# Windowed attention and a Strassen-type maxout layer on one core: the order of the attention groups on TensorE, a pinned instruction order, and later subtractions

## The chip, the core and the metric

One NeuronCore of a Trainium2 chip runs the whole program. The metric is the device time of one execution in microseconds (us), the median of several runs; for the kernel before it is 850.38 us (three runs, 847.42 to 852.41).

The engines are named as in the profile: PE is TensorE (matmuls and transposes), PEld its weight loads, DVE is VectorE, ACT is ScalarE, POOL is GpSimd, SP issues DMAs. PSUM is the memory into which PE writes and from which DVE and ACT read; POOL works on SBUF alone.

## The reference

Batch 8, 8 heads, 576 positions, head size 64; then 4608 tokens, model width 512, hidden width 768.

```python
def _attn_ref(q, k, v):
    scores = scale * np.matmul(q, k.transpose(0, 1, 3, 2))
    bias = slopes[:, None, None] * (-np.abs(rel).astype(np.float32))[None, :, :]
    mask = (rel >= 0) & (rel < window)          # window = 128
    scores = np.where(mask, scores + bias[None], -1000000000.0)
    attn = np.exp(scores - np.max(scores, axis=-1, keepdims=True))
    attn = attn / (np.sum(attn, axis=-1, keepdims=True) + 1e-09)
    return np.matmul(attn, v)

def _moe_ref(x, w1, w2, w3, w_out):             # x: heads side by side, (B*S, 512)
    h = np.maximum(np.maximum(x @ w1, x @ w2), x @ w3)
    return h @ w_out
```

## The kernel before, in words

**Attention.** A task is one batch and one pair of heads, and has five blocks of queries, four of 128 rows and one of 64. Two consecutive blocks form a group. For a group PE does three kinds of work. `products` (L248 to L264) writes the scores into the PSUM tile `ps_s`, in matmuls of 64 rows by 64 columns of the array, four side by side. `turn` (L314 to L342) transposes the normalised probabilities `p` into the PSUM tile `pt`, in the full 128x128 array (64x128 for the block of 64 rows). `mix` (L344 to L370) multiplies with v into `ps_x`, in 128x64 pieces side by side (64x64 for the block of 64 rows); blocks 0 and 1 make one run of `mix`, blocks 2, 3 and 4 the other. Between them DVE merges the two halves of the window and adds the bias (L277, L289), ACT takes the exponential and normalises (L293, L312), ACT copies `pt` out of PSUM (L325, L331, L334), and POOL cuts the copy into the two triangles (L335, L339). So PE gets ten groups in a batch.

**The maxout layer.** Each of the 11 products of a batch (9 for the three weight matrices, 2 for the output) is done by a scheme with 7 multiplications of blocks instead of 8, in two-part (high and low) arithmetic. One such multiplication is a unit (`unit`, L482 to L522), 77 in a batch: 6 matmuls of 128x128 by 288 columns for the first 63, 9 for the 14 of the output. They are all issued at L510. Units write to three PSUM buffers `ps_m` in turn, which DVE (L468, L473, L476) and ACT (L519) empty.

When the three matrices of a third `p` of the hidden layer are done, `factors_h` (L420 to L450) forms the differences of its blocks for the output product: a subtraction on DVE (`sub`, L391) and a `cut` into high and low part, a cast on ACT (L387) and a subtraction on POOL (L388). For the third part DVE does the first two. The last subtraction, `sub(b10, b10, t)` at L449, overwrites b10, and so waits until POOL has finished the cut of b10 that L448 asked for.

**Order.** The code makes a list of events, each with a time in steps of attention (L525 to L578), and issues them sorted by time. A `mix` stands at .01 of its step, a `turn` at .02, a `products` at .03. `later` (L379) puts the steps of `factors_h` on a list by unit number, and `unit` issues those that are due. Behind that stands a scheduler: it takes the issued instructions and sets a fixed order for each engine by its own estimate of when operands are ready, so an instruction may come to stand earlier or later than it was issued.

**Weights.** They are prepared during batch 0, kept in DRAM and streamed from there in later batches (`stream`, L216), through a ring of two buffers for each half, by DMAs that POOL issues (L221).

Of the kernel before, what the change touches and what calls it, by code (L numbers as in the profile page):

```python
# [18 lines left out]
LAG_T, LAG_X = 4, 6  # L19
# [10 lines left out]
def attention_maxout_kernel(  # L30
# [11 lines left out]
    nc = tc.nc  # L42
# [7 lines left out]
    NB = (S + P - 1) // P  # L50
# [165 lines left out]
    def stream():  # L216
        nonlocal streamed
        n, a = divmod(streamed, 2)
        if n < 9 * B and prepared == 120 and ahead(n, a):
            place(n, a)  # L220
            nc.gpsimd.dma_start(wts[n, a], keep[n % 9][a])  # L221
            streamed += 1


    tasks = [(b, hp) for b in range(B) for hp in range(NP)]
    qkt, vt = {}, {}
# [21 lines left out]
    def products(s):  # L248
        whole = s < NP * NB and s % 4 == 2
        ps = [ps_m.tile([P, 512], F32, name=f"ps_m{j}") for j in range(2)] if whole else [scores[:, j] for j in range(2)]  # L250
        for a, (t, i) in enumerate(steps[s:s + 2]):
            n = rows[i]
            banks[t, i] = [x[:, a * 2 * P:(a + 1) * 2 * P] for x in ps], None if whole else a
            for j in range(2):
                for d in range(0, n, D):
                    q0 = i * P + d
                    k0, k1 = (0, P) if i == 0 else ((i - 1) * P, i * P + n) if whole else (q0 - P, q0 + D)
                    o = a * 2 * P + k0 - (i - 1) * P
                    nc.tensor.matmul(  # L259
                        ps[j][d:d + D, o:o + k1 - k0],  # L260
                        lhsT=qkt[t][j * D:(j + 1) * D, 0, q0:q0 + D],
                        rhs=qkt[t][j * D:(j + 1) * D, 1, k0:k1],
                        start=True, stop=True, skip_group_check=True,
                    )  # L264

    def score(t, i):
        b, hp = tasks[t]
# [46 lines left out]
    def turn(s):  # L314
        pt = ps_t.tile([P, 2, 2, P], F32, name="pt")
        two = steps[s:s + 2]
        for a, (t, i) in enumerate(two):
            n = rows[i]
            p = pn.pop((t, i))
            for j in range(2):  # L320
                nc.tensor.transpose(out=pt[:, a, j, :n], in_=p[:n, j], identity=ident[:n, :n])  # L321
        r = s_p.tile([P, 2, 2, P], F32, name="pr", bufs=2)
        whole = all(i and rows[i] == P for _, i in two)
        if whole:
            nc.scalar.copy(out=r, in_=pt)  # L325
        for a, (t, i) in enumerate(two):
            n = rows[i]
            w = pp_p.tile([P, 2, 2, P], F32, name="pp")
            pp[t, i] = w
            if i == 0:  # L330
                nc.scalar.copy(out=w[:, :, 0, :n], in_=pt[:, a, :, :n])  # L331
                continue
            if not whole:
                nc.scalar.copy(out=r[:, a, :, :n], in_=pt[:, a, :, :n])  # L334
            nc.gpsimd.affine_select(  # L335
                out=pp[t, i - 1][:, :, 1, :n], in_=r[:, a, :, :n], pattern=[[0, 2], [-1, n]],
                compare_op=ALU.is_gt, fill=0.0, base=0, channel_multiplier=1,
            )
            nc.gpsimd.affine_select(  # L339
                out=w[:n, :, 0, :n], in_=r[:n, a, :, :n], pattern=[[0, 2], [1, n]],  # L340
                compare_op=ALU.is_ge, fill=0.0, base=0, channel_multiplier=-1,
            )  # L342

    def mix(t, i):  # L344
        b, hp = tasks[t]
        if i == 0:
            xp[t] = ps_x.tile([P, 1024], F32, name="ps_x")
        x, vv, w = xp[t], vt[t], pp[t, i]
        n = rows[i]
        m = rows[i + 1] if i + 1 < NB else 0  # L350
        parts = []
        c0 = i * P
        if m == 0 or (c0 // 512 != (c0 + P) // 512):
            parts.append((0, n, c0))
            if m:
                parts.append((P, P + m, c0 + P))
        else:
            parts.append((0, P + m, c0))
        for a, e, c in parts:
            for j in range(2):  # L360
                nc.tensor.matmul(  # L361
                    x[j * D:(j + 1) * D, c:c + e - a],
                    lhsT=vv[:n, i, j * D:(j + 1) * D],
                    rhs=w[:n, j].rearrange("p a b -> p (a b)")[:, a:e],
                    start=i == 0 or (c % 512 == 0 and a == P), stop=True, skip_group_check=True,
                )
        if i == NB - 1:
            if hp % 2 == 0:
                xk[b, hp // 2] = xk_p.tile([P, 2, S], F32, name=f"xk{hp // 2}")
            nc.scalar.copy(out=xk[b, hp // 2][:, hp % 2], in_=x[:, :S])  # L370
# [8 lines left out]
    def later(when, what, *args):  # L379
        todo.append((when, what, args))  # L380
        todo.sort(key=lambda x: x[0])
# [38 lines left out]
    def factors_h(b, p, ij, when):  # L420
        b00, b01, b10, b11 = [hq.get((p, x)) for x in ((0, 0), (0, 1), (1, 0), (1, 1))]

        def cut(k, src):
            if p < 2:
                if p == 0:
                    hs[b, k] = hs_p.tile([P, 2, 2, C], F32R, name="hs")
                t = hs[b, k][:, p]
            else:
                if k in (0, 2, 4, 5):
                    hs[b, "at"] = hs_p.tile([P, 2, 2, C], F32R, name="hs2", bufs=4)  # L430
                t = hs[b, k, 2] = hs[b, "at"][:, k in (1, 3, 6)]
            split((t[:, 0], t[:, 1]), src, nc.vector if p == 2 and k < 2 else nc.gpsimd)

        if ij == (0, 0):
            t = hq["t", p] = t_p.tile([P, C], F32, name="t")
            sub(t, b01, b00)
            later(when, cut, 0, b00)
            later(when, cut, 1, t)
        elif ij == (1, 1):
            t = hq["t", p]  # L440
            later(when, sub, t, b11, t)
            later(when, sub, b01, b11, b01)
            later(when, cut, 2, t)
            later(when, cut, 3, b11)
        elif ij == (1, 0):
            t = hq["t", p]
            later(when, cut, 5, b01)
            later(when, cut, 4, b10)  # L448
            later(when, sub, b10, b10, t)  # L449
            later(when, cut, 6, b10)  # L450

# [30 lines left out]
    def unit(u):  # L482
# [24 lines left out]
            part_of[n, k] = ps_m.tile([P, 512], F32, name=f"ps_m{u % 3}")[:, :C]  # L507
        ps = part_of[n, {2: 0, 5: 0, 6: 0, 3: 1}.get(k, k)]
        for i, (lt, rt) in enumerate(pairs):
            nc.tensor.matmul(  # L510
                ps, lhsT=lt, rhs=rt, start=i == 0 and k in (0, 1, 4), stop=i == len(pairs) - 1,
                skip_group_check=True,
            )
        if g < 9:
            used.add((at, k))
        stream()
# [11 lines left out]
    def at(when, what, *args):  # L528
        events.append((when, len(events), what, args))
# [3 lines left out]
    for t, (b, hp) in enumerate(tasks):  # L533
        for i in range(NB):
# [7 lines left out]
            c = s - (t * NB + i) % 2  # L542

            if s == c:
                at(c + LAG_T + 0.02, turn, t * NB + i)
                at(c + 0.03, products, t * NB + i)
            at(s + 0.04, score, t, i)
            if i % 2 or i + 1 == NB:
                at(s + 0.9, sums_of, t, i)
                at(s + 1.3, normalise, t, i)  # L550
            e = t * NB + next(min(e + 1, NB - 1) for e in GROUPS if e >= i)
            at(e - e % 2 + shift[b] + LAG_X + 0.01, mix, t, i)

    ready = [n_steps * (b + 1) - 2 + LAG_X + 0.05 + shift[b] for b in range(B)]
    when = ready[0]
# [13 lines left out]
    for s in range(1, n_steps + LAG_X):  # L569
        at(s + 0.2, weights, 2)  # L570

    load(0)
    nc.sync.dma_start(ident, c_ident)
    slopes(0)
# [42 lines left out]
```

## Time and profile before

| what | value |
|---|---|
| median of the runs | 850.38 us |
| the profiled execution | 846.03 us, of which the span of the program's instructions is 844.3 us |
| busy share of the span | PE 92%, PEld 80%, DVE 68%, ACT 64%, POOL 37% |
| mean granted clock of TensorE | 0.961 |
| instructions | 17942, of them 6272 matmuls |
| moved by DMA | 184.78 MB, 219 GB/s |

The span falls into three parts: to about 195 us attention of batch 0, preparation of the weights and the first units; then six batches of about 94.4 us, in which a batch's units run beside the next batch's attention; and from about 766 us the last batch's units alone.

In the timeline a row merges instructions of one line that follow each other: start, time from the first start to the last end, engine, line, operation, tiles, the form of the first of them, and their number. Matmuls overlap in their ends, so the time of a section is read as the difference of two rows' starts. The scores are multiplied in two passes, so that 8 instructions of the order are 16 in the trace; the same holds for `mix`. A bracket at the end of a row is the idle time before it, with what ended it.

### The profile page before, as it was taken

To read this page: it belongs to the slowest core of one execution; us is meant where nothing else is said; L and a number is where in the kernel's file an instruction comes from. 1 tells how busy PE (TensorE), PEld (TensorE's weight loads), DVE (VectorE), ACT (ScalarE), POOL (GpSimd) and SP (SyncE) were. 2 spreads that over 40 slices of the span, in tenths; PEclk is the share of its full clock that TensorE was granted. 3 is DMA by queue.
4 is the path that set the end of the run, shared out by engine and by line. 5 is a ranking of instruction groups with operands and counts; after the bars stand their busy time and mean duration, and the time that the engine had idled before them with its cause. 6 is when DMAs were issued, how large, how long until landed. Compare 5 with 4: busy or idle time off the path is not lost.

```text
span 844.3 us, 17942 instructions
## 1 busy us (share of the span) xinstructions
PE 780.3 (92%) x6272; PEld 674.3 (80%) x6272; DVE 570.0 (68%) x1830; ACT 544.5 (64%) x1790; POOL 310.3 (37%) x544
## 2 busy tenths in 40 slices
PE   4767778799999999999999999999999999999997
PEld 2335666589888988888888988889888988889897
DVE  5788989996666845775557845775657846583552
ACT  6898888876666856676556756675657756642332
POOL 1212141442354415452345415451345415440431
PEclk9865989799999999999999999999999999999999
DMA  6742568673887558873787558873787557764851
GB/s 230 278 168 70 220 230 305 210 257 125 262 277 249 195 171 261 277 253 118 239 273 252 196 175 267 275 255 110 245 281 240 194 187 244 230 223 153 296 205 56
DMA packets 43401, 184.78 MB, mean 219 GB/s; under 512 B 4784, under 2 KB 13744, under 8 KB 34096
## 3 DMA queue, kind: packets, MB, share of 16 engines
q0 software_dynamic: 18144, 115.61, 41.7%
q1 hardware_dynamic: 25024, 67.97, 22.8%
q8 instruction: 49, 0.80, 0.4%
q14 instruction: 40, 0.33, 0.1%
q10 hardware_dynamic: 144, 0.07, 0.0%
HBM read 157.68 MB, written 25.95 MB: 217 GB/s over the span
## 4 chain that ended last, share of the span: by engine, by line
PE 68%; DVE 8%; issue 8%; POOL 6%; ACT 6%; DMA 3%; SPq 0%; POOLq 0%; ACTq 0%; DVEq 0%
PE ps_m L510 53%; PE ps_x L361 6%; PE ps_s L259 5%; PE pt L321 4%; POOL hs L388 3%; DMA wt<-keep 2%; POOL pp L339 1%; POOL pp L335 1%; ACT p L293 1%; ACT hs L387 1%; DVE hs L158 1%; DVE t L473 1%; DMA hs<-in_w_all 1%; DVE hs L144 1%; DVE xs L388 1%
## 5 line engine op out<-in xcount | busy, mean ns | idle before, releaser
L510 PE MATMUL ps_m<-xs,wt 128*128 128x288 f32 x3024 | 440.8, 302 | 19.9 <-DVE hq L476 7.6
L510 PEld LDWEIGHTS ps_m<-xs,wt 128*128 128x128 f32 x3024 | 414.6, 191 | 46.6 <-issue 12.2
L519 ACT COPY t<-ps_m 128x288 f32<-128x288 f32 x264 | 101.2, 392 | 92.3 <-PE ps_m L510 91.9
L335 POOL TENSOR_SCALAR_AFFINE_SELECT pp<-pr 128x256 f32<-128x256 f32 (+1 forms) x128 | 53.9, 421 | 263.0 <-ACT pr L334 175.9
L510 PE MATMUL ps_m<-hs,ow 128*128 128x288 f32 x1008 | 144.5, 299 | 3.2 <-POOL hs L388 2.4
L293 ACT ACTIVATE p<-s,st 128x128 f32<-128x128 f32 (+1 forms) x320 | 126.7, 399 | 27.9 <-DVE st L289 27.2
L510 PEld LDWEIGHTS ps_m<-hs,ow 128*128 128x128 f32 x1008 | 136.0, 188 | 9.6 <-POOL hs L388 5.9
L388 POOL TENSOR_TENSOR hs<-hq,hs 128x288 fp32r<-128x288 f32 x112 | 101.3, 914 | 88.3 <-ACT hs L387 88.1
L221 POOL DMA_DIRECT2D wt<-keep x126 | 69.8, 554 | 150.3 <-PE ps_m L510 148.8
L312 ACT ACTIVATE p<-p,st 128x128 f32<-128x128 f32 (+1 forms) x320 | 108.6, 399 | 20.6 <-DVE st L305 20.0
L289 DVE CUSTOM_DVE_ANT_0 s<-ps_s,bias 128x128 f32<-128x128 f32 (+1 forms) x300 | 77.5, 283 | 25.9 <-PE ps_s L259 19.0
L473 DVE TENSOR_TENSOR t<-ps_m,t 128x288 f32<-128x288 f32 x144 | 65.1, 453 | 43.5 <-PE ps_m L510 27.3
L361 PE MATMUL ps_x<-pp,v 128*64 128x256 f32 (+3 forms) x768 | 85.6, 338 | 7.3 <-POOL pp L335 6.6
L277 DVE COPY_PREDICATED ps_s<-prev,ps_s 128x256 f32<-128x256 uint8 x120 | 50.6, 421 | 56.9 <-PE ps_s L259 55.7
L259 PE MATMUL ps_s<-qk 64*64 64x192 f32 (+1 forms) x1080 | 71.3, 346 | 11.5 <-DVE st L289 7.4
L321 PE MATMUL pt<-ident,p 128*128 128x128 f32 (+1 forms) x320 | 62.0, 295 | 17.3 <-ACT p L312 15.2
L387 ACT CAST hs<-hq 128x288 fp32r<-128x288 f32 x120 | 50.3, 433 | 39.0 <-DVE hq L474 26.0
L361 PEld LDWEIGHTS ps_x<-pp,v 128*64 128x64 f32 (+1 forms) x768 | 46.7, 140 | 35.1 <-POOL pp L335 11.8
L321 PEld LDWEIGHTS pt<-ident,p 128*128 128x128 f32 (+1 forms) x320 | 37.2, 145 | 42.7 <-ACT p L312 20.9
L474 DVE TENSOR_TENSOR hq<-t,hq 128x288 f32<-128x288 f32 x144 | 67.4, 475 | 2.7
L259 PEld LDWEIGHTS ps_s<-qk 64*64 64x64 f32 x1080 | 40.1, 141 | 26.9 <-issue 13.2
L293 ACT ACTIVATION_READ_ACCUMULATOR p<-s,st 128x1 f32 (+1 forms) x320 | 61.5, 192 | 0.0
(56 smaller groups left out, 719.2 us busy)
## 6 DMA issues: line engine op xcount, KB each, us to landing
wt<-keep POOLq DMA_DIRECT2D x63, 1024.0 KB, 7.2
wt<-keep POOLq DMA_DIRECT2D x63, 768.0 KB, 4.6
qk<-in_qk SPq DMA_DIRECT2D x31, 576.0 KB, 5.8
hs<-in_w_all SPq DMA_DIRECT2D x24, 512.0 KB, 6.6
v<-in_v SPq DMA_DIRECT2D x32, 320.0 KB, 4.8
keep<-wt SPq DMA_DIRECT2D x9, 1024.0 KB, 4.7
outT<-t SPq DMA_DIRECT2D x64, 144.0 KB, 1.8
keep<-wt SPq DMA_DIRECT2D x9, 768.0 KB, 5.2
```

The source lines that it names most:

```text
L221: nc.gpsimd.dma_start(wts[n, a], keep[n % 9][a])
L259: nc.tensor.matmul(ps[j][d:d + D, o:o + k1 - k0], lhsT=qkt[t][j * D:(j + 1) * D, 0, q0:q0 + D], rhs=qkt[t][j * D:(j + 1) * D, 1, k0:k1], s ...
L289: nc.vector.tensor_tensor_reduce(out=s[:n], in0=ps[j][:n, P:2 * P], in1=(bias if i else bias0)[:n, 2 * hp + j, :], scale=-0.125, scalar=3. ...
L293: nc.scalar.activation(p[:n, j], s[:n], AF.Exp, bias=st[:n, 0, a, j:j + 1], scale=-1.0, accum_out=st[:n, 1, a, j:j + 1])
L312: nc.scalar.activation(p[:n, j], p[:n, j], AF.Copy, scale=st[:n, 2, a, j:j + 1])
L321: nc.tensor.transpose(out=pt[:, a, j, :n], in_=p[:n, j], identity=ident[:n, :n])
L361: nc.tensor.matmul(x[j * D:(j + 1) * D, c:c + e - a], lhsT=vv[:n, i, j * D:(j + 1) * D], rhs=w[:n, j].rearrange("p a b -> p (a b)")[:, a:e ...
L388: e.tensor_tensor(out=lo, in0=src, in1=hi.bitcast(F32), op=ALU.subtract)
L473: nc.vector.tensor_tensor(out=s, in0=ps, in1=e, op=ALU.add)
L474: nc.vector.tensor_tensor(out=h, in0=s, in1=h, op=ALU.max)
L510: nc.tensor.matmul(ps, lhsT=lt, rhs=rt, start=i == 0 and k in (0, 1, 4), stop=i == len(pairs) - 1, skip_group_check=True,)
L519: nc.scalar.copy(out=e, in_=ps)
```

## The change

It has three parts. First, from the step in which batch 2's products with v begin, every PE instruction is tied to the one issued before it (`tc.keep_in_program_order`), so the scheduler can't move it. Second, the times of the attention events are changed: within a step, `mix` comes at .001, `products` at .002, `turn` at .003, so that the transposes follow the scores. Third, in `factors_h` the differences and cuts of block (1,1) are issued 2 units later for the first two thirds, and the last subtraction and its cut 5 units later (2 for the last third). The matmuls themselves, their number and their shapes don't change.

```diff
+    fixed = False
+
+    def pe(ins):
+        if fixed:
+            tc.keep_in_program_order(ins)
...
         elif ij == (1, 1):
             t = hq["t", p]
+            when += 2 * (p < 2)
             later(when, sub, t, b11, t)
...
             later(when, cut, 5, b01)
             later(when, cut, 4, b10)
+            when += 5 if p < 2 else 2
             later(when, sub, b10, b10, t)
             later(when, cut, 6, b10)
...
             if s == c:
-                at(c + LAG_T + 0.02, turn, t * NB + i)
-                at(c + 0.03, products, t * NB + i)
+                at(c + 0.002, products, t * NB + i)
+                at(c + LAG_T + 0.003, turn, t * NB + i)
...
-            at(e - e % 2 + shift[b] + LAG_X + 0.01, mix, t, i)
+            at(e - e % 2 + shift[b] + LAG_X + 0.001, mix, t, i)
...
+    def fix():
+        nonlocal fixed
+        fixed = True
+
+    at(2 * n_steps + LAG_X + shift[2], fix)
```

All `nc.tensor` calls of `products`, `turn`, `mix` and `unit` are wrapped in `pe(...)`. The lines of the changed kernel are numbered 6 to 13 higher: scores L265, transposes L327, products with v L367, units L518, subtraction L397.

What it moves, engine by engine, is seen in two places of batch 4. The first is PE around the sixth run of `mix` in that batch, before:

```order
L510 MATMUL ps_m_7363<-xs,wt_7203 128x288 x6
L361 MATMUL ps_x<-pp,v 64x256
L510 MATMUL ps_m_7229<-xs,wt_7156 128x288 x6
L510 MATMUL ps_m_7352<-xs,wt_7203 128x288 x6
L510 MATMUL ps_m_7363<-xs,wt_7203 128x288 x6
L510 MATMUL ps_m_7421<-xs,wt_7266 128x288 x6
L361 MATMUL ps_x<-pp,v 64x256
L361 MATMUL ps_x<-pp,v 64x128 x2
L361 MATMUL ps_x<-pp,v 64x64 x4
L321 MATMUL pt<-ident,p 128x128 x4
L259 MATMUL ps_s<-qk 64x128 x4
L259 MATMUL ps_s<-qk 64x192 x4
```

And the same place in the changed kernel:

```order
L518 MATMUL ps_m_7229<-xs,wt_7156 128x288 x6
L518 MATMUL ps_m_7346<-xs,wt_7203 128x288 x6
L518 MATMUL ps_m_7357<-xs,wt_7203 128x288 x6
L518 MATMUL ps_m_7418<-xs,wt_7266 128x288 x6
L367 MATMUL ps_x<-pp,v 64x256 x2
L367 MATMUL ps_x<-pp,v 64x128 x2
L367 MATMUL ps_x<-pp,v 64x64 x4
L265 MATMUL ps_s<-qk 64x128 x4
L265 MATMUL ps_s<-qk 64x192 x4
L327 MATMUL pt<-ident,p 128x128 x4
L518 MATMUL ps_m_7346<-xs,wt_7266 128x288 x6
```

The first product with v no longer stands four units ahead of its seven companions, and the transposes stand behind the scores. The swap of transposes and scores is the same in every group from batch 1's on.

The second place is DVE where the last subtraction of the first third stands (`hq_6821<-hq_6821,t_6969`; the three rows at L476 empty the next units' `ps_m` buffers), before:

```order
L289 ISA s_7122,st_7121<-ps_s_105,bias0_115 128x128
L289 ISA st_7121 128x1
L289 ISA s_7125,st_7121<-ps_s_105,bias0_115 128x128
L391 TENSOR_TENSOR hq_6821<-hq_6821,t_6969 128x288
L476 TENSOR_TENSOR hq_7099<-ps_m0_7013,t_7085 128x288
L476 TENSOR_TENSOR hq_7108<-ps_m1_7101,t_7009 128x288
L302 TENSOR_SCALAR st_7062<-st_7062 64x2
L476 TENSOR_TENSOR hq_7118<-ps_m2_7002,t_7020 128x288
L305 RECIPROCAL st_7062<-st_7062 64x2
```

In the changed kernel:

```order
L295 ISA s_7118,st_7117<-ps_s_105,bias0_115 128x128
L295 ISA st_7117 128x1
L295 ISA s_7121,st_7117<-ps_s_105,bias0_115 128x128
L308 TENSOR_SCALAR st_7062<-st_7062 64x2
L311 RECIPROCAL st_7062<-st_7062 64x2
L397 TENSOR_TENSOR hq_6821<-hq_6821,t_6969 128x288
L484 TENSOR_TENSOR hq_7095<-ps_m0_7005,t_7081 128x288
L484 TENSOR_TENSOR hq_7104<-ps_m1_7097,t_7001 128x288
L484 TENSOR_TENSOR hq_7114<-ps_m2_6994,t_7012 128x288
```

The subtraction is issued five units later, but the scheduler, which DVE is still left to, has put it back ahead of the same three rows; only the two small operations on `st` have moved ahead of it. In batch 0 the order on DVE, ACT and POOL changes in more places.

More of the change, by code (lines that the diff above doesn't have):

```diff
@@ L258, in products @@
                     o = a * 2 * P + k0 - (i - 1) * P
-                    nc.tensor.matmul(
+                    pe(nc.tensor.matmul(
                         ps[j][d:d + D, o:o + k1 - k0],
@@ L263, in products @@
                         start=True, stop=True, skip_group_check=True,
-                    )
+                    ))
     def score(t, i):
@@ L320, in turn @@
             for j in range(2):
-                nc.tensor.transpose(out=pt[:, a, j, :n], in_=p[:n, j], identity=ident[:n, :n])
+                pe(nc.tensor.transpose(out=pt[:, a, j, :n], in_=p[:n, j], identity=ident[:n, :n]))
         r = s_p.tile([P, 2, 2, P], F32, name="pr", bufs=2)
@@ L360, in mix @@
             for j in range(2):
-                nc.tensor.matmul(
+                pe(nc.tensor.matmul(
                     x[j * D:(j + 1) * D, c:c + e - a],
@@ L365, in mix @@
                     start=i == 0 or (c % 512 == 0 and a == P), stop=True, skip_group_check=True,
-                )
+                ))
         if i == NB - 1:
@@ L509, in unit @@
         for i, (lt, rt) in enumerate(pairs):
-            nc.tensor.matmul(
+            pe(nc.tensor.matmul(
                 ps, lhsT=lt, rhs=rt, start=i == 0 and k in (0, 1, 4), stop=i == len(pairs) - 1,
                 skip_group_check=True,
-            )
+            ))
         if g < 9:
```

## The prediction

> **What bounds the kernel now.** First the busy time by engine and the windows by stage (window, its length, busy us and instructions of PE, PEld, DVE, ACT, POOL, granted clock, DMA share, GB/s): batch 0's second half, one of the six like batches, the end.
>
> ```profile
> PE 780.3 (92%) x6272; PEld 674.3 (80%) x6272; DVE 570.0 (68%) x1830; ACT 544.5 (64%) x1790; POOL 310.3 (37%) x544
> ```
>
> ```profile
> 100.00:195.00 95.00, 80.75 (x600) 65.00 (x601) 89.84 (x271) 76.86 (x238) 32.19 (x50) 0.89 0.69 248
> ...
> 478.80:573.20 94.40, 92.77 (x785) 82.35 (x786) 61.32 (x203) 60.53 (x206) 38.91 (x70) 1.00 0.70 228
> 753.50:844.30 90.80, 83.18 (x606) 81.02 (x606) 41.11 (x84) 27.26 (x69) 26.67 (x37) 1.00 0.53 177
> ```
>
> In the like batch PE is busy 92.8 of 94.4 us at full clock, and no other engine passes 65%. So PE sets the period, and only two things can shorten it: its waits, and whatever its instructions cost beyond their work. The waits of PE in that batch are two:
>
> ```profile
> PE ps_m L510 <- DVE hq L476: 1.4, 1, 1.4
> PE ps_m L510 <- POOL hs L388: 0.2, 1, 0.2
> ```
>
> For the other cost, PE's timeline in the same batch. The sections are x (L361), t (transposes, L321), s (scores, L259), u (units, L510); differences of starts are what counts.
>
> ```profile
> 508.13 6.66 PE L510 MATMUL ps_m<-xs,wt 128*128 128x288 f32 x48
> 514.72 1.25 PE L361 MATMUL ps_x<-pp,v 128*64 128x256 f32 x16
> 515.90 0.66 PE L321 MATMUL pt<-ident,p 128*128 128x128 f32 x4
> 516.48 0.76 PE L259 MATMUL ps_s<-qk 64*64 64x192 f32 x12
> 517.17 3.46 PE L510 MATMUL ps_m<-xs,wt 128*128 128x288 f32 x24
> 522.03 3.46 PE L510 MATMUL ps_m<-xs,wt 128*128 128x288 f32 x24 [1.40 <-DVE hq L476]
> ...
> 535.72 3.46 PE L510 MATMUL ps_m<-xs,wt 128*128 128x288 f32 x24
> 539.11 0.65 PE L361 MATMUL ps_x<-pp,v 128*64 128x256 f32 x2
> 539.69 3.45 PE L510 MATMUL ps_m<-xs,wt 128*128 128x288 f32 x24
> 543.07 1.24 PE L361 MATMUL ps_x<-pp,v 128*64 128x256 f32 x14
> 544.24 0.66 PE L321 MATMUL pt<-ident,p 128*128 128x128 f32 x4
> ...
> 553.24 0.65 PE L321 MATMUL pt<-ident,p 128*128 128x128 f32 x4
> 553.82 0.88 PE L259 MATMUL ps_s<-qk 64*64 64x192 f32 x16
> 554.63 5.86 PE L510 MATMUL ps_m<-xs,wt 128*128 128x288 f32 x42
> 560.42 1.25 PE L361 MATMUL ps_x<-pp,v 128*64 128x256 f32 x16
> ```
>
> 48 units take 6.59 us (508.13 to 514.72) and 42 take 5.79 (554.63 to 560.42), so one more unit matmul costs 0.80 / 6 = 0.133 us.
>
> **The swap of transposes and scores.** The trace holds the new neighbours too, in places where the scheduler happened to make them: x followed by s (the page shows 14 and 2 of x, 14 and 2 of s, mingled), and t followed by u.
>
> ```profile
> 183.01 1.19 PE L361 MATMUL ps_x<-pp,v 128*64 128x256 f32 x14
> ...
> 184.09 0.82 PE L259 MATMUL ps_s<-qk 64*64 64x192 f32 x14
> 184.84 2.68 PE L510 MATMUL ps_m<-hs,ow 128*128 128x288 f32 x18
> ```
>
> ```profile
> 733.14 0.66 PE L321 MATMUL pt<-ident,p 128*128 128x128 f32 x4
> 733.55 5.84 PE L510 MATMUL ps_m<-xs,wt 128*128 128x288 f32 x42
> 739.32 1.08 PE L361 MATMUL ps_x<-pp,v 128*64 128x256 f32 x8
> ...
> 741.24 0.65 PE L321 MATMUL pt<-ident,p 128*128 128x128 f32 x4
> 741.81 5.87 PE L510 MATMUL ps_m<-xs,wt 128*128 128x288 f32 x42
> ```
>
> Four transposes take 0.58 us when scores follow (515.90 to 516.48) and 0.41 when units follow (733.14 to 733.55). Both transposes and units are of the form 128*128; every change of form seems to cost. Now a group with 16 x. Before: x 1.18, t 0.58, s (16 of them, 553.82 to 554.63) 0.81, together 2.57. After: x and s without anything between, 183.01 to 184.84, 1.83; then t 0.41; together 2.24. That saves 0.33; the 42 units behind save 0.02 more (5.77 behind t, 5.79 behind s). So 0.35 for a group of this kind, of which a batch has three. Where x has 8 instructions it ends in the form 128*64, s follows with a change of form as t did before, and only the exit of t is saved: 0.17 + 0.02 = 0.19, two in a batch. Where t ends with the block of 64 rows, its exit costs 0.57 before units (741.24 to 741.81) as 0.58 before scores (553.24 to 553.82): nothing. The groups without x, and the one with units between x and t, gain under 0.1 each, and I leave them out. The sum for a batch is 3 x 0.35 + 2 x 0.19 = 1.43 us.
>
> [...]
>
> **The pinning.** Unit order in the like batches stays as it was; what goes is the x that ran four units early: 539.11 to 544.24 is 5.13 us for 16 x and 24 units. Unsplit they cost 1.18 + 24 x 0.133 = 4.37. That saves 0.76 in each of batches 2 to 6. What pinning could cost is a wait that the scheduler had dodged; in these rows no t, s or x waited, so I take zero, and as bound the largest wait of the like batch, 1.4 us.
>
> **The later subtractions.** The wait of 1.40 us at 522.03 comes from DVE; here are DVE, POOL and ACT at that place:
>
> ```profile
> 516.01 0.64 ACT L370 COPY xk<-ps_x 128x576 f32<-128x576 f32 x1 [0.70 <-PE ps_x L361]
> ...
> 516.55 0.43 ACT L387 CAST hs<-t 128x288 fp32r<-128x288 f32 x1
> ...
> 517.07 1.04 POOL L388 TENSOR_TENSOR hs<-t,hs 128x288 fp32r<-128x288 f32 x1 [1.14 <-ACT hs L387]
> ...
> 519.57 1.55 POOL L388 TENSOR_TENSOR hs<-hq,hs 128x288 fp32r<-128x288 f32 x2
> ...
> 521.15 0.46 DVE L391 TENSOR_TENSOR hq<-hq,t 128x288 f32<-128x288 f32 x1 [1.62 <-POOL hs L388]
> 521.53 0.82 DVE L476 TENSOR_TENSOR hq<-ps_m,t 128x288 f32<-128x288 f32 x2
> ```
>
> The subtraction (L449) stands on DVE ahead of L476, waits 1.62 us for POOL's cut of the same block, and L476 queued behind it is what PE waits for. Issued later it would let L476 pass. But the scheduler has put it back ahead of the three L476 (the order in the change's section), so I count this part at zero in the like batches. The wait stays, and it does more: POOL's chain starts from ACT's copy of x (516.01), that is from the end of x, and runs on without a gap. It ends when it ended before, counted from x; the 0.35 us that PE gains behind this x is only added to the wait. So one of the three groups gives nothing.
>
> The group at 560.42 I treat the same way. Behind it the cuts of the last third end late, and PE waits for them:
>
> ```profile
> 563.30 0.50 POOL L335 TENSOR_SCALAR_AFFINE_SELECT pp<-pr 128x256 f32<-128x256 f32 x1 [3.58 <-ACT pr L334]
> ...
> 567.68 2.32 POOL L388 TENSOR_TENSOR hs<-hq,hs 128x288 fp32r<-128x288 f32 x2
> ...
> 570.06 1.85 PE L510 MATMUL ps_m<-hs,ow 128*128 128x288 f32 x12 [0.18 <-POOL hs L388]
> ```
>
> POOL begins there when ACT has copied the transposes, which now come about 0.65 us later (x, then 0.69 of scores). One cut has moved ahead of that in POOL's order, which makes about as much good. I take another 0.35 as lost, with a bound of 0.65 more lost on the one side, nothing lost on the other.
>
> **The sum.** A full batch: 1.43 + 0.76 - 2 x 0.35 = 1.49 us; batches 2 to 5, 4 x 1.49 = 6.0. Batch 1 has no split x, 0.73. Batch 6 has half the groups: 2 x 0.19 + 0.35 + 0.76 - 0 for the group that only feeds the wait, 1.5. I add 0.6 for the groups left out, 6 x 0.1. Together 8.8 us, and 844.3 becomes 835.5. Batch 0 is bound by DVE (89.84 of 95 us), which does the same work in another order: zero, and as bound on either side one hole like the largest there, 4.26 us (its row stands under (c)). In the end (from 753.5) the order is the same, and waits on weights don't depend on what came before: zero. The profiled execution, 846.03 us, would take 837.2; the median of the runs shown is 4.35 above that execution, so 850.38 x 835.5 / 844.3 gives **841.5 us**.
>
> **The rivals.** (a) The DVE wait goes after all. If the small operations that moved ahead of the subtraction, or the cuts' new order, let it start without waiting, PE loses neither the wait nor the groups' gain: 24 units take 4.86 us from 517.17 to 522.03 and 3.39 from 535.72 to 539.11, 1.5 us, in six batches 9, and 2 x 0.35 in each, 4: 841.5 - 13 = 828.5. For it: the issue is later. Against it: the place in DVE's order, and POOL's gapless chain. 0.12.
>
> (b) New waits eat the rest. Scores come earlier and transposes later, so DVE's merge (L277) can stand before an operation that frees a `ps_m` buffer, and POOL's chain at 563 starts later. With 0.65 for the latter and half of the 1.4 bound for the former, 1.3 us a batch over five is 6.5, and the time 848. For it: DVE's order has such swaps. Against it: a buffer is needed again only two units later, 1.6 us. 0.22.
>
> (c) Slower: batch 0 loses more than the rest gains. PE waited there for ACT, and its clock fell:
>
> ```profile
> 156.86 3.25 PE L510 MATMUL ps_m<-xs,wt 128*128 128x288 f32 x12 [4.26 <-ACT t L519]
> ```
>
> ```profile
> 150.00:165.00 15.00, 9.94 (x56) 7.25 (x55) 14.74 (x40) 11.67 (x35) 8.67 (x13) 0.66 0.49 173
> ```
>
> Twelve matmuls take 3.25 us there where 12 x 0.133 is 1.6; with the idle time one such hole costs 4.26 + 1.65 = 5.9. Reordered work on DVE and ACT can make holes. It decides from the third more: 3 x 5.9 - 8.8 = +9, 859.5. Against it: PE's order there is nearly unchanged, and DVE has the same work. 0.06. [...]
>
> (d) The order does not save what I read from single rows, and only the split x counts: 5 x 0.76 = 3.8, 846.5. Against it: the rows repeat to 0.01 us. 0.07.
>
> **How the numbers follow.** The forecast has 0.53. The range reaches to (a) below and past (b) above: 829 to 851. A measurement here can tell about 0.5%, 4.3 us, from no change. Faster than 846.1: the forecast, (a), and a third of (b) and of (d): 0.53 + 0.12 + 0.10 = 0.75. Within: the rest of (b) and (d), 0.19. Slower: 0.06.
>
> **What would show it.** In the new timeline t of 0.41 before units, x and 16 s together 1.83, no x of two; a period near 92.9 us; a wait on L484 of about 1.7 us, with the subtraction before it on DVE waiting 1.6 us for POOL. Wrong would be: that wait gone (a); a period above 94 with new waits on `ps_m` (b); a first batch that ends more than 6 us later with a lower clock (c); t before units at 0.58 (d).

## The result, and the profile after

The changed kernel takes 838.98 us (median of four runs, 836.86 to 839.13), the kernel before 849.24 (four runs, 847.42 to 852.41). The ratio is 0.9869, 95% interval 0.9833 to 0.9905: faster by 1.3%. The profiled execution took 838.98 us with a span of 837.3, against 846.03 and 844.3.

A batch has 504 unit matmuls, so the 1st, 505th, 1009th of them and so on mark the batches in any of the traces. By these marks the 7.0 us between the two spans divide as follows. (The forecast had 0.6 us more, for the groups it left out, which it didn't divide. Of the six batches called alike, only 2 to 5 take 94.4 us each.)

| stretch | before, us | after, us | saved | foretold |
|---|---|---|---|---|
| start of the span to batch 0's first unit | 74.42 | 75.58 | -1.2 | 0 |
| batch 0 (to batch 1's first unit) | 131.51 | 134.49 | -3.0 | 0 |
| batch 1 | 96.08 | 94.61 | 1.5 | 0.7 |
| batches 2 to 5 | 377.81 | 368.25 | 9.6 | 6.0 |
| batch 6 | 87.66 | 86.90 | 0.8 | 1.5 |
| batch 7 to the end | 76.86 | 77.45 | -0.6 | 0 |

The windows of batches 2 to 5, before and then after (same columns as in the prediction), show that the time came out of PE's busy time: it fell from 371.2 to 362.0 us, while PE's idle time went from 6.6 to 6.2.

```profile
302.00:679.80 377.80, 371.21 (x3138) 329.51 (x3137) 245.49 (x809) 242.10 (x825) 155.89 (x276) 1.00 0.69 228
```

```profile
304.70:672.90 368.20, 362.00 (x3138) 326.53 (x3137) 237.65 (x809) 240.09 (x825) 149.96 (x276) 1.00 0.70 234
```

Of PE's waits in that stretch one is left: the one on POOL is gone, the one on DVE stands.

```profile
PE ps_m L518 <- DVE hq L484: 5.4, 4, 1.4
```

PE's timeline in batch 4. The sections are named as in the prediction: x are the products with v, t the transposes, s the scores, u the units; a group is an x, t and s that stand together, and "8 x" or "16 x" says how many instructions its x has. As in the prediction, "48 units" means 48 matmuls of units, that is 8 whole units. Of before, the rows that the prediction doesn't show and that are compared below (x L361, t L321, s L259, u L510):

```profile
496.61 1.25 PE L361 MATMUL ps_x<-pp,v 128*64 128x256 f32 x16
...
499.08 6.66 PE L510 MATMUL ps_m<-xs,wt 128*128 128x288 f32 x48
505.67 1.08 PE L361 MATMUL ps_x<-pp,v 128*64 128x256 f32 x8
...
525.34 0.60 PE L321 MATMUL pt<-ident,p 128*128 128x128 f32 x4
...
562.87 2.68 PE L510 MATMUL ps_m<-hs,ow 128*128 128x288 f32 x18
...
571.75 0.60 PE L321 MATMUL pt<-ident,p 128*128 128x128 f32 x4
```

After (x L367, s L265, t L327, u L518):

```profile
494.60 1.19 PE L367 MATMUL ps_x<-pp,v 128*64 128x256 f32 x14
495.54 0.33 PE L265 MATMUL ps_s<-qk 64*64 64x128 f32 x2
495.62 0.22 PE L367 MATMUL ps_x<-pp,v 64*64 64x64 f32 x2
495.68 0.71 PE L265 MATMUL ps_s<-qk 64*64 64x128 f32 x14
496.32 0.66 PE L327 MATMUL pt<-ident,p 128*128 128x128 f32 x4
496.74 6.64 PE L518 MATMUL ps_m<-xs,wt 128*128 128x288 f32 x48
503.31 1.08 PE L367 MATMUL ps_x<-pp,v 128*64 128x256 f32 x8
...
514.49 3.85 PE L518 MATMUL ps_m<-xs,wt 128*128 128x288 f32 x24
519.69 3.46 PE L518 MATMUL ps_m<-xs,wt 128*128 128x288 f32 x24 [1.34 <-DVE hq L484]
523.07 0.88 PE L265 MATMUL ps_s<-qk 64*64 64x192 f32 x16
...
533.19 7.01 PE L518 MATMUL ps_m<-xs,wt 128*128 128x288 f32 x48
540.13 1.19 PE L367 MATMUL ps_x<-pp,v 128*64 128x256 f32 x14
...
557.09 1.19 PE L367 MATMUL ps_x<-pp,v 128*64 128x256 f32 x14
...
559.22 2.66 PE L518 MATMUL ps_m<-hs,ow 128*128 128x288 f32 x18
...
567.59 0.88 PE L265 MATMUL ps_s<-qk 64*64 64x192 f32 x16
```

A group with 16 x takes 494.60 to 496.74, 2.14 us, where it took 2.47 (496.61 to 499.08). The 48 units that hold the wait for DVE take 514.49 to 523.07, 8.58, where they took 8.17 (517.17 to 525.34). The last group with 16 x and the 60 units behind it, most of them of the output, take 557.09 to 567.59, 10.50, where they took 560.42 to 571.75, 11.33.

### The profile page after: what moved, and what is told of

It is laid out like the page before. It is cut to its first block, busy times and chain, and to the rows that moved or that the text cites. A ratio compares the mean times of both kernels' runs of the same rounds, so it can differ in the third digit from the quotient of the medians.

```text
span 837.3 us, 17958 instructions
## 1 busy us (share of the span) xinstructions
PE 770.6 (92%) x6272; PEld 673.2 (80%) x6272; DVE 560.9 (67%) x1830; ACT 541.1 (65%) x1790; POOL 303.7 (36%) x544
## 4 chain that ended last, share of the span: by engine, by line
PE 63%; DVE 12%; issue 9%; POOL 7%; ACT 5%; DMA 3%; SPq 0%; POOLq 0%; DVEq 0%; ACTq 0%
PE ps_m L518 47%; PE ps_x L367 6%; PE ps_s L265 5%; POOL hs L394 5%; PE pt L327 4%; DMA wt<-keep 2%; DVE t L481 1%; DVE wt L169 1%; ACT p L299 1%; POOL pp L345 1%; DVE hq L482 1%; POOL pp L341 1%; DVE hs L144 1%; DVE xs L394 1%; DVE hs L158 1%
## 5 line engine op out<-in xcount | busy, mean ns | idle before, releaser
L518 PE MATMUL ps_m<-xs,wt 128*128 128x288 f32 x3024 | 441.0, 302 | 23.7 <-DVE hq L484 9.3
L518 PEld LDWEIGHTS ps_m<-xs,wt 128*128 128x128 f32 x3024 | 416.0, 192 | 35.8 <-DVE hq L484 11.5
L518 PE MATMUL ps_m<-hs,ow 128*128 128x288 f32 x1008 | 143.1, 298 | 4.1 <-POOL hs L394 2.4
L518 PEld LDWEIGHTS ps_m<-hs,ow 128*128 128x128 f32 x1008 | 136.0, 188 | 7.0 <-POOL hs L394 3.3
L394 POOL TENSOR_TENSOR hs<-hq,hs 128x288 fp32r<-128x288 f32 x112 | 95.5, 861 | 100.0 <-ACT hs L393 99.9
L367 PE MATMUL ps_x<-pp,v 128*64 128x256 f32 (+3 forms) x768 | 83.2, 341 | 5.2 <-POOL pp L341 4.4
L265 PE MATMUL ps_s<-qk 64*64 64x192 f32 (+1 forms) x1080 | 73.5, 345 | 12.3 <-DVE st L295 7.8
L327 PE MATMUL pt<-ident,p 128*128 128x128 f32 (+1 forms) x320 | 63.6, 302 | 17.1 <-ACT p L318 15.6
L327 PEld LDWEIGHTS pt<-ident,p 128*128 128x128 f32 (+1 forms) x320 | 36.1, 147 | 49.8 <-ACT p L318 21.5
L367 PEld LDWEIGHTS ps_x<-pp,v 128*64 128x64 f32 (+1 forms) x768 | 46.2, 142 | 32.7 <-issue 10.3
L482 DVE TENSOR_TENSOR hq<-t,hq 128x288 f32<-128x288 f32 x144 | 69.5, 486 | 2.8
L265 PEld LDWEIGHTS ps_s<-qk 64*64 64x64 f32 x1080 | 42.4, 141 | 30.6 <-issue 10.8
L340 ACT COPY pr<-pt 128x256 f32<-128x256 f32 x64 | 19.0, 322 | 72.4 <-PE pt L327 72.3
```

The source lines that it names most:

```text
L265: pe(nc.tensor.matmul(ps[j][d:d + D, o:o + k1 - k0], lhsT=qkt[t][j * D:(j + 1) * D, 0, q0:q0 + D], rhs=qkt[t][j * D:(j + 1) * D, 1, k0:k1] ...
L327: pe(nc.tensor.transpose(out=pt[:, a, j, :n], in_=p[:n, j], identity=ident[:n, :n]))
L367: pe(nc.tensor.matmul(x[j * D:(j + 1) * D, c:c + e - a], lhsT=vv[:n, i, j * D:(j + 1) * D], rhs=w[:n, j].rearrange("p a b -> p (a b)")[:, ...
L394: e.tensor_tensor(out=lo, in0=src, in1=hi.bitcast(F32), op=ALU.subtract)
L482: nc.vector.tensor_tensor(out=h, in0=s, in1=h, op=ALU.max)
L518: pe(nc.tensor.matmul(ps, lhsT=lt, rhs=rt, start=i == 0 and k in (0, 1, 4), stop=i == len(pairs) - 1, skip_group_check=True,))
```

## The experiments

All numbers are read by the marks above. "Batch 0" is the stretch from the first unit to batch 1's first, "period" the mean of batches 2 to 5, "end" from batch 7's first unit. The ratios, with 95% intervals, are to the kernel before as it ran beside each (medians from 849.2 to 850.4); batch 0, period and end are from one profiled execution of each kernel. In the experiments' rows the lines of the code have other numbers, as each changes the code.

| kernel | median, us | ratio | batch 0 | period | end |
|---|---|---|---|---|---|
| before | 849.24 | 1 | 131.5 | 94.45 | 76.9 |
| changed | 838.98 | 0.9869 (0.9833 to 0.9905) | 134.5 | 92.06 | 77.5 |
| order alone | 839.36 | 0.9880 (0.9842 to 0.9918) | 133.3 | 92.40 | 76.1 |
| pin alone | 846.44 | 0.9964 (0.9944 to 0.9984) | 131.8 | 94.08 | 77.5 |
| late alone | 849.13 | 1.0006 (0.9979 to 1.0033) | 137.1 | 93.76 | 77.0 |
| without late | 837.78 | 0.9865 (0.9829 to 0.9902) | 132.6 | 92.02 | 77.9 |
| turn first | 839.35 | 0.9884 (0.9850 to 0.9917) | 133.3 | 92.39 | 77.7 |
| tail free | 838.19 | 0.9867 (0.9827 to 0.9906) | 131.9 | 92.37 | 78.2 |
| cut back | 850.51 | 1.0013 (0.9984 to 1.0042) | 133.2 | 93.95 | 76.9 |
| sub behind | 835.72 | 0.9838 (0.9807 to 0.9869) | 134.1 | 91.55 | 77.0 |
| combined | 833.95 | 0.9805 (0.9765 to 0.9845) | 133.6 | 91.30 | 77.2 |
| behind from 1 | 834.09 | 0.9787 (0.9750 to 0.9824) | 133.2 | 91.77 | 77.3 |
| behind, cuts | 830.02 | 0.9764 (0.9745 to 0.9784) | 131.9 | 90.75 | 76.9 |

### The three parts, one by one

Two theories stood against each other. The first: the order saves only through changes of form, the last third's later subtraction removes the wait for POOL behind the output units, and the order costs the front (all up to batch 1's first unit) its 4 us. The second gives the removal of the wait to the order and the front's loss to the later subtractions.

The order alone, on the kernel before:

```diff
-                at(c + LAG_T + 0.02, turn, t * NB + i)
-                at(c + 0.03, products, t * NB + i)
+                at(c + 0.002, products, t * NB + i)
+                at(c + LAG_T + 0.003, turn, t * NB + i)
...
-            at(e - e % 2 + shift[b] + LAG_X + 0.01, mix, t, i)
+            at(e - e % 2 + shift[b] + LAG_X + 0.001, mix, t, i)
```

> The kernel before with the new times of mix, products and turn alone (no pin, no later subtractions). Compared by two stretches of the trace: the front (from the span's start to the 505th unit matmul, the first of batch 1; before 205.93 us, after 210.07) and the period of a like batch (before 94.43, after 92.0). Theory 1: the order brings about 1.5 us a batch through the changes of form and nothing more, because the 0.33 before the output units is taken back by the wait for POOL's cuts: period 92.9 to 93.2; and the order is what costs the front 4 us: front near 210; time about 3 us below before, ratio 0.996. Theory 2: the order also removes the wait for POOL's cuts behind the output units, and the front's loss comes from the later subtractions: period 92.4, front near 206, ratio 0.988.

Measured: period 92.40, 2.05 less than before, with the 60 units of the output at 8.37 us (before 8.87): the wait goes with the order, as the second theory had it. The front takes 209.4 us, as the first theory had it; but 1.7 of the 3.4 more than before lie ahead of the first unit, a stretch that takes from 74.0 to 76.4 us in the thirteen traces.

The pin alone (`fix` and `pe(...)` on the kernel before):

> The kernel before with the pin from batch 2 on alone. Both theories: the x of two instructions no longer runs ahead, 0.75 us a batch, so a period of 93.7 from batch 2 on, front unchanged at 206, time 3.8 us below before, ratio 0.9955. If instead the pinned order brings a new wait behind the joined x, as in the changed kernel (0.34), the period is 94.0 and the ratio 0.9975.

Measured: a period of 94.02 from batch 3 on. The x that ran ahead is now joined to the rest of its run and saves what was foretold, but the 48 units ahead of it take 6.87 us where 48 units behind another group take 6.59: the new small wait. Net 0.4 us a batch.

The later subtractions alone (the two lines with `when +=` on the kernel before):

> The kernel before with the later subtractions alone. Theory 1: the last third's subtraction, two units later, is what removes the waits for POOL's cuts behind the output units (0.5 us a batch): period 93.9, front 206, ratio 0.996. Theory 2: the later subtractions do nothing in the like batches (94.4) and cost the front 4 us: front 210, ratio 1.005.

Measured: the period falls to 93.76 and batch 0 grows to 137.1, so each theory has one half. But the 0.7 us are not behind the output units (8.88 there, as before). They are at the wait for DVE, where the 48 units take 7.39 instead of 8.17. DVE there:

```profile
524.61 0.45 DVE L478 TENSOR_TENSOR hq<-ps_m,t 128x288 f32<-128x288 f32 x1
...
526.34 0.46 DVE L391 TENSOR_TENSOR hq<-hq,t 128x288 f32<-128x288 f32 x1 [0.78 <-POOL hs L388]
526.72 0.45 DVE L478 TENSOR_TENSOR hq<-ps_m,t 128x288 f32<-128x288 f32 x1
```

One of the three operations that empty `ps_m` has got past the subtraction. With the new order it doesn't (the order in the change's section), so the effect shouldn't be in the changed kernel. The test takes the later subtractions out of it:

```diff
-            when += 2 * (p < 2)
-            when += 5 if p < 2 else 2
```

> The changed kernel without the later subtractions (order and pin stay). Theory 1: period 92.5 (0.5 above the changed kernel), front 210 as in the changed kernel, time about 3 us above it, ratio to before 0.991. Theory 2: period 92.0 as in the changed kernel, front 206, time about 4 us below it, ratio 0.982.

Measured: 92.02 and 837.78 us, no different from the changed kernel. In it the later subtractions are worth nothing. The front takes 207.9 us, between the two theories' 210 and 206, and settles neither.

### Which property of the order counts

Transposes first, then products with v, then scores; no later subtractions:

```diff
-                at(c + LAG_T + 0.003, turn, t * NB + i)
+                at(c + LAG_T + 0.0005, turn, t * NB + i)
```

> Order and pin as in the changed kernel, no later subtractions, but the transposes ahead of the products with v instead of behind the scores: transposes, products with v, scores. The changes of form in a batch are as many as with the transposes last (34, before 46). Theory A: the number of changes between forms is what counts (units and transposes share one form, products with v run on into scores): the period is that of the same kernel with the transposes last, 92.0 us, within 0.3. Theory B: the gain comes from where the scores stand (DVE gets them 0.6 us earlier) or the transposes stand: the scores now come as late as before, the period is 93.5 to 94.0 as with the pin alone.

```profile
401.11 0.60 PE L327 MATMUL pt<-ident,p 128*128 128x128 f32 x4
...
409.84 0.38 PE L327 MATMUL pt<-ident,p 128*128 128x128 f32 x2
```

Group and 48 units take 401.11 to 409.84, 8.73 us; with the transposes last 494.60 to 503.31, 8.71; before 496.61 to 505.67, 9.06. For the group theory A holds: what counts is that x runs into s and t stands beside units, on whichever side. Theory B's 93.5 doesn't come. Two of the four periods are 92.1, near the 92.0 with the transposes last; the other two, 92.5 and 92.8, lose 0.3 to 0.6 us more among the units (in batch 4 to a wait for weights) and put the mean at 92.39, a little outside theory A's bound. That even the first two come so near is partly chance, since where the transposes stand does set when DVE, ACT and POOL can start: the 48 units that wait for DVE take 7.61 us there, not 8.58, and the 60 units behind the last group with 16 x take 9.25, not 8.37, and the two nearly cancel.

### The end

The pin taken off again for the last batch, without the later subtractions:

```diff
+    at(ready[B - 1], fix, False)
```

> Order and pin, no later subtractions, and the pin taken off again at the first unit of the last batch. Theory A: the pin costs the end 0.7 to 1.5 us, because PE must wait there for weights where the scheduler let output units pass: from the first unit of the last batch to the end 76.1 to 76.9 us instead of 77.93; time 1 to 1.8 us below the kernel that keeps the pin (837.8). Theory B: the end depends on where the weights' transfers fall, not on the pin: 77.5 to 78, no difference.

Theory A fell: 78.2 us against 77.9. What the end takes (76.1 to 78.2 in all thirteen traces) doesn't follow the pin: without it at the end, five traces lie between 76.1 and 78.2, with it, eight between 76.9 and 77.9. Its waits for weights (`wt<-keep`) add up to anything from 0.7 to 3.8 us. The period of 92.37 comes from one batch of 93.55, whose 1.5 us more aren't explained here; the other three take 91.9 to 92.0.

### The wait behind the output units

In the changed kernel POOL does this after the last group with 16 x, which starts at 557.09 and whose units start at 559.22:

```profile
560.03 0.81 POOL L394 TENSOR_TENSOR hs<-hq,hs 128x288 fp32r<-128x288 f32 x1 [3.64 <-ACT hs L393]
560.82 0.62 POOL L341 TENSOR_SCALAR_AFFINE_SELECT pp<-pr 128x256 f32<-128x256 f32 x1
561.39 0.92 POOL L345 TENSOR_SCALAR_AFFINE_SELECT pp<-pr 128x256 f32<-128x256 f32 x1
562.29 0.80 POOL L394 TENSOR_TENSOR hs<-t,hs 128x288 fp32r<-128x288 f32 x1
563.05 1.32 POOL L394 TENSOR_TENSOR hs<-hq,hs 128x288 fp32r<-128x288 f32 x1
...
564.90 0.82 POOL L394 TENSOR_TENSOR hs<-hq,hs 128x288 fp32r<-128x288 f32 x1
```

The cut of block (1,1) runs first, in time in which POOL would wait for the transposes; before, it came after both selects, and ahead of the cut of `t` (the row at 564.48 in the last section). The same order on POOL stands in the kernel with the new order alone, so it is the order that moved the cut. The experiment ties that one cut back, behind the cut of `t`, which is one place further back than it had before:

```diff
-            split((t[:, 0], t[:, 1]), src, nc.vector if p == 2 and k < 2 else nc.gpsimd)
+            (tc.keep_in_program_order if p == 2 and k == 3 else id)(split((t[:, 0], t[:, 1]), src, nc.vector if p == 2 and k < 2 else nc.gpsimd))
```

> The changed kernel with one subtraction of POOL tied back: the cut of block (1,1) in the last third, which the scheduler had put ahead of the two selects behind the products with v, stands behind them and the cut of t again; PE, ACT and SP keep their order. Theory A: this one place on POOL is why the 60 units behind the last joined group take 8.37 us instead of 8.87: they take 8.8 to 9.2 again, the period is 92.4 to 92.8 instead of 92.05, five batches 2 to 4 us, ratio to before 0.990 to 0.992. Theory B: POOL's chain ends earlier because it starts earlier, the place of this cut doesn't matter: 8.4 and 92.05, ratio 0.987.

PE and then POOL in that kernel, whose group starts at 558.89:

```profile
561.02 2.66 PE L518 MATMUL ps_m<-hs,ow 128*128 128x288 f32 x18
...
565.58 2.74 PE L518 MATMUL ps_m<-hs,ow 128*128 128x288 f32 x18 [0.31 <-POOL hs L394]
569.50 1.88 PE L518 MATMUL ps_m<-hs,ow 128*128 128x288 f32 x12 [1.17 <-POOL hs L394]
571.30 0.39 PE L265 MATMUL ps_s<-qk 64*64 64x192 f32 x4
```

```profile
562.37 1.33 POOL L341 TENSOR_SCALAR_AFFINE_SELECT pp<-pr 128x256 f32<-128x256 f32 x1 [4.18 <-ACT pr L340]
...
564.04 1.48 POOL L394 TENSOR_TENSOR hs<-t,hs 128x288 fp32r<-128x288 f32 x1
565.49 2.60 POOL L394 TENSOR_TENSOR hs<-hq,hs 128x288 fp32r<-128x288 f32 x2
...
568.64 0.80 POOL L394 TENSOR_TENSOR hs<-hq,hs 128x288 fp32r<-128x288 f32 x1
```

Theory A holds, and its price was too low: the 60 units take 561.02 to 571.30, 10.28 us, and every other section of the batch is the changed kernel's to 0.06. The period is 93.95. POOL does the same work in both, but from the start of its first operation to the end of the fourth cut it takes 5.69 us in the changed kernel (560.03 to 565.72) and 7.07 with the cut tied back (562.37 to 569.44). So between the first place and the last, one instruction on an engine that is busy 36% of the changed kernel's span is worth 1.9 us a batch, and with it last the change brings nothing that can be measured (1.0013). The place that it had before, one ahead of the last, wasn't run in the new order. The profiled execution, 844.38 us, is the shortest of this kernel's ten (to 855.36); where the others spent more isn't seen.

### The wait for DVE

The changed kernel with the subtraction of the first two thirds queued behind the operation that was last issued to empty `ps_m`:

```diff
+    def behind(*a):
+        with tc.issue_after(last["put"].ins): sub(*a)
...
-            later(when, sub, b10, b10, t)
+            later(when, behind if p < 2 else sub, b10, b10, t)
...
-            nc.vector.tensor_tensor(out=h, in0=ps, in1=e, op=ALU.add)
+            last["put"] = nc.vector.tensor_tensor(out=h, in0=ps, in1=e, op=ALU.add)
```

> The changed kernel with the last subtraction of the first two thirds queued on DVE behind the subtraction that empties ps_m and was issued last before it; nothing else on DVE or POOL is tied. Theory A: PE's wait in the first third is only that this subtraction stands ahead of the three that empty ps_m: the 48 units there take 6.6 us again instead of 8.6, those behind the joined x in the second third 6.6 instead of 6.94; period 89.8 to 90.5, six batches 10 to 12 us, time 827 to 829. Theory B: POOL or ACT hold PE up at the same place when DVE doesn't: the wait shrinks by less than half, period over 91, time over 833.

DVE at the place of the wait, PE there, and PE's waits from 300 to 660 us:

```profile
515.43 0.82 DVE L484 TENSOR_TENSOR hq<-ps_m,t 128x288 f32<-128x288 f32 x2
516.42 0.46 DVE L484 TENSOR_TENSOR hq<-ps_m,t 128x288 f32<-128x288 f32 x1 [0.17 <-PE ps_m L518]
516.87 0.46 DVE L397 TENSOR_TENSOR hq<-hq,t 128x288 f32<-128x288 f32 x1
```

```profile
512.54 7.03 PE L518 MATMUL ps_m<-xs,wt 128*128 128x288 f32 x48
519.50 0.88 PE L265 MATMUL ps_s<-qk 64*64 64x192 f32 x16
...
524.50 4.23 PE L518 MATMUL ps_m<-xs,wt 128*128 128x288 f32 x30 [1.14 <-DMA wt<-keep]
```

```profile
PE ps_m L518 <- DMA wt<-keep: 4.1, 3, 1.6
```

The wait for DVE is gone, as theory A has it: 6.96 us for the 48 units instead of 8.58. What theory A said of the second third fell (6.93, not 6.6), and so did its time: 835.7 lies where theory B had it, though not for its reason. One period is 90.41; the other three (91.7 to 92.2) give the gain to a new wait, for weights. POOL, which issues those transfers, was busy when this one was due:

```profile
515.27 1.56 POOL L394 TENSOR_TENSOR hs<-hq,hs 128x288 fp32r<-128x288 f32 x2
516.79 0.58 POOL L221 DMA_DIRECT2D wt<-keep  x1
```

It is issued 29.8 us into the batch in all four. In the batch of 90.41 it takes 5.4 us to land, and PE doesn't wait; in the other three it takes 7.6 to 8.1.

The parts put together, with the old order up to batch 1's attention, no later subtraction in batch 0, and no pin in the last batch:

```diff
-            when += 2 * (p < 2)
+            when += 2 * (p < 2 and b > 0)
-            when += 5 if p < 2 else 2
+            when += (5 if p < 2 else 2) * (b > 0)
...
+                at(c + (0.002 if b > 1 else 0.03), products, t * NB + i)
+                at(c + LAG_T + (0.003 if b > 1 else 0.02), turn, t * NB + i)
...
+            at(e - e % 2 + shift[b] + LAG_X + (0.001 if b > 1 else 0.01), mix, t, i)
```

> Together: new order from batch 2's attention on, later subtractions from batch 1 on, the last subtraction of the first two thirds behind those that empty ps_m, the pin from batch 2 to the first unit of the last batch. Theory A (each part's effect stands by itself): from the first unit to batch 1's first 131.5 to 131.8 us as before instead of 134.5, period 90.0, the last batch 76.1 to 76.9: time 822 to 825. Theory B (the front's loss isn't from order and subtractions in batch 0, or the gains overlap): 828 or more.

Measured: 833.95 us; batch 0 at 133.6 even with the old order and without the later subtractions, so theory A's front fell, and three of four periods (91.3 to 91.9) again hold waits. The next pair keeps the new order and the pin throughout; the second of them takes two cuts off POOL:

```diff
-            later(when, behind if p < 2 else sub, b10, b10, t)
+            later(when, behind if p < 2 and b else sub, b10, b10, t)
...
-            split((t[:, 0], t[:, 1]), src, nc.vector if p == 2 and k < 2 else nc.gpsimd)
+            split((t[:, 0], t[:, 1]), src, nc.vector if p == 2 and k < 2 or p == 0 and k in (4, 5) else nc.gpsimd)
```

> The kernel with the subtraction queued behind those that empty ps_m, but the later subtractions (and that tie) from batch 1 on only; the new order everywhere, the pin from batch 2 to the end. Theory A: the later subtractions in batch 0 cost about 2 of the 3 us that the stretch from the first unit to batch 1's first lost (before 131.5 and 131.8, order alone 131.9 to 133.3 in three runs, with the later subtractions 134.1 and 134.5): 132 to 133.3 us there, time 1 to 2 us below 835.7. Theory B: the new order alone costs them, 134 or more.

> As the kernel beside it, and of the first third the cuts of blocks (0,1) and (1,0) subtract on DVE (0.46 us each) instead of POOL (0.8). Theory A: with the subtraction's wait gone PE waits for weights because POOL issues their transfers late, behind its cuts: with 1.6 us of cuts off POOL in that place, the waits on wt<-keep in batches 2 to 6 (4.1 us in three places before) fall to under 1.5, every like batch takes 90.3 to 90.6 us instead of 90.4 to 92.2, time 2.5 to 4 us below the kernel beside it. Theory B: the transfers themselves are what is late (they share the DMA engines with the loads of q, k and v, and take 7 us): the waits stay, periods between 91 and 92, no difference.

The first: batch 0 at 133.2, time 834.09; both within theory A, though the 1.6 us against 835.7 lie inside the intervals, and the 0.9 us of batch 0 inside the spread of single traces. The second: no wait on `wt<-keep` is left in batches 2 to 6, all four periods lie between 90.65 and 90.92, and what is left of PE's waits from 300 to 660 us is

```profile
PE ps_m L518 <- ACT t L527: 1.6, 4, 0.4
```

Theory A again, with periods up to 0.3 above its range. That transfer is now issued 28.7 us into the batch, 1.1 sooner, and PE doesn't wait although it takes 7.2 to 7.6 us to land; so when it is issued and how long it takes decide together, and theory B is right that the transfer's own length counts. From 500 to 530 us of the kernel with the subtraction queued behind, the weights' queue took 73.0% of the time of the 16 DMA engines and the queue of the loads of q, k and v 7.8%; whether the loads lengthen the transfers isn't tested. The 4.1 us between the two medians aren't clear of noise (their intervals overlap); the periods, 91.2 to 92.0 and then 90.7 to 90.9, don't overlap. At 830.02 us, ratio 0.9764 (0.9745 to 0.9784), this kernel beats both the kernel before and the changed one, whose whole interval (0.9833 to 0.9905) lies above.

## Why the prediction was right, and where it wasn't

**What bounds the kernel, and the swap.** PE does, and the swap saved what its rows said. Per group: 0.33 for 16 x (foretold 0.35), 0.17 for two of the groups with 8 x (0.19), nothing for the other two, whose t ends with the block of 64 rows (nothing), 0.11 for the two without x (left out as under 0.1). The group itself takes 2.47 and then 2.14, not 2.57 and 2.24, and x with its scores 1.72, not 1.83: the forecast added scores of 192 columns times 16, and no group with 16 x has those. The difference is the same. One count was off: the batch has four groups with 16 x, not three, since the split one gains too once it is joined. Its 0.33 was eaten by the new wait ahead of it, 6.94 us for 48 units instead of 6.60, the cost that the pinning was said not to have. So the split group with its units brought 0.73, close to the 0.76, but by luck: out of three terms, of which two cancel.

**The wait of 1.40.** Right: the subtraction stays ahead, the wait stays and takes in what PE gains ahead of it (the 48 units grew by 0.41, the group saved 0.32). That it is DVE's order that holds it was only argued then; queueing the subtraction behind the three operations showed it. Rival (a), the wait going, needs that, and would not have given its 13 us even so (835.7 us, not 828.5): the weights are late next.

**The group at 560.42.** This is the step that failed. It said that POOL's later start costs another 0.35, with up to 0.65 more, and that a cut that moved ahead "makes about as much good". In the trace the group gained 0.32 and the 60 units behind it 0.50 more: 0.8 a batch instead of 0, nearly all of the 0.9 by which the batch came out better than 1.49 (2.39). POOL does start later against the units, 0.81 us behind their start (560.03 and 559.22) instead of 0.43 (563.30 and 562.87), but it ends its fourth cut sooner, 6.50 us behind it instead of 7.13. So the cut that moved made good more than the later start cost; tied back to the last place it costs 1.9. Rival (b)'s mechanism, POOL's chain starting later, is real: with the cut last it is the result.

**The pinning.** Alone it saves 0.4 a batch, not 0.76; its bound of 1.4 held.

**The later subtractions.** Zero in the like batches of the changed kernel, as foretold. Alone, in the old order, they save 0.7 there.

**Batch 0 and the end.** Zero was wrong by 3.0 and 0.6, the 3.0 within the 4.26 that was set as bound for batch 0. Another 1.2 went ahead of the first unit, no more than that stretch varies. How the 3.0 divide isn't settled. Batch 0 takes 131.5 and 131.8 in two traces with the same instructions there, 131.9 to 133.3 in six with a new order and no later subtraction, 133.2 to 134.5 in three with both, 137.1 with the later subtractions alone, and 133.6 with neither in the combined kernel. So the subtractions may cost one or two, which single traces can't show; the rest is no more than the spread. The holes of rival (c) didn't come: the clock granted in batch 0 is 0.88 before and 0.89 after.

```profile
74.00:206.00 132.00, 112.49 (x825) 93.30 (x822) 120.36 (x366) 104.88 (x322) 39.04 (x61) 0.88 0.60 214
```

```profile
75.00:210.00 135.00, 112.55 (x824) 94.41 (x821) 120.51 (x367) 104.89 (x324) 38.10 (x58) 0.89 0.60 210
```

**Batch 6.** 0.8 instead of 1.5, because there PE's wait for POOL grew, from 0.5 to 1.1 us.

**The median.** The span came out at 837.3 for a forecast of 835.5. That it lies so near is partly luck: batches 2 to 5 gave 3.6 us more than foretold, and the start, batch 0 and the end took 4.8 that were set at zero. That the median is still below the 841.5 comes from the scaling: before's profiled execution lay 4.35 us below the median of the runs then shown, after's lies on it.

**Rival (d)** is out: t ahead of units takes 0.42 (496.32 to 496.74), where its row had 0.41.

## What to carry to other kernels

Where sections of several array forms share TensorE, try an order in which neighbours have one form: here a group with 16 x and the 48 units behind it went from 9.06 to 8.71 us. What a swap can save can be read from the same section before different neighbours: here four transposes took 0.58 us before scores and 0.41 before units. When such a swap shifts work on the main engine, follow the chain of work on every other engine that starts from it, instruction by instruction: here the place of one cut on POOL could decide whether the swap paid (a period of 92.06 us with it first, of 93.95 with it last). And expect a removed wait to uncover another, so take them off together: here PE waited 5.4 us for DVE in batches 2 to 5, then 4.1 for the weights and then 1.6 for ACT from 300 to 660 us.

## What the runs showed of the hardware

Beside each other, a cut on POOL and DVE's operations with two inputs from SBUF don't both keep their times in these rows: one or the other grows. The cut of 0.80 us (so at 566.33) took 1.88 before (POOL), while DVE did two such (DVE, 564.58 to 565.69, 1.11 us):

```profile
564.48 1.88 POOL L388 TENSOR_TENSOR hs<-hq,hs 128x288 fp32r<-128x288 f32 x1
566.33 0.80 POOL L388 TENSOR_TENSOR hs<-t,hs 128x288 fp32r<-128x288 f32 x1
```

```profile
564.58 0.45 DVE L391 TENSOR_TENSOR hq<-hq 128x288 f32<-128x288 f32 x1
564.95 0.74 DVE L391 TENSOR_TENSOR xt<-xk,xt 128x576 f32<-128x576 f32 x1
```

0.80 + 1.11 is 1.91, near the 1.88. In the changed kernel the same cut takes 0.81 (560.03), and it is the first of these two DVE operations that grows, from 0.45 to 0.65:

```profile
560.52 0.65 DVE L397 TENSOR_TENSOR hq<-hq 128x288 f32<-128x288 f32 x1
```

That is probably why the cut, run earlier and beside other work of DVE, gains more than its place in the queue; no run tests it by itself.

The two orders with 34 changes of form a batch give 8.71 and 8.73 us for a group with 16 x and the 48 units behind it, the one with 46 gives 9.06: with fewer changes they take less time. Products with v and scores, both in 64*64 at the seam, run mingled (495.54 to 495.68): together they take 1.72 us (494.60 to 496.32), where with t between them they took 1.18 and 0.70 (496.61 to 497.79, 498.38 to 499.08).
